# Attention scores: both row maxima of a head pair in one half step, and the next pair's score products ahead of the value products

## The chip, the cores and the metric

The kernel runs on one core of a Trainium2 chip. The metric is device time in microseconds (us) from start to end of one execution. Three executions of the kernel before took 997.72, 998.46 and 1002.0 us, so the median is 998.46 us. A fourth one was recorded by the hardware profiler, and all rows below come from it.

## The reference, cut to what matters

Three blocks follow one another: attention with a learned bias on the scores, a mixture of experts, and a dense layer with a squared ReLU. The change lies in the attention alone:

```python
# 4 batches, 8 heads, 576 positions, head size 64
scores = q @ k.T / sqrt(64) + bias[head]      # 576 x 576 for each batch and head
scores = scores - scores.max(-1)
attn = exp(scores); attn = attn / (attn.sum(-1) + 1e-9)
x = attn @ v                                  # goes on to the experts
```

## The kernel before, in words

A unit of work is a tile of 128 query rows, one batch and one pair of heads (for the last 64 rows of a batch, two batches share a tile). There are 72 units. For each unit TensorE (PE) makes four sorts of products, and three other steps lie between them:

- `emit_qk` (line 484): the score products of both heads, 12 of them for a full tile, into two PSUM tiles named `ps_s`, one for each head. The pool of these tiles holds two, so the next unit's score products cannot start before both tiles have been read.
- `emit_max` (L496), on VectorE (DVE): it reads one `ps_s`, adds the bias, writes the sum to an SBUF tile `ssb` and takes the row's extremum `mn` (with the sign turned, so that it is the row maximum of the scores). One instruction and a short read of the accumulator for each head.
- `emit_exp` (L509), on ScalarE (ACT): the exponential, from `ssb` to `pr`, one for each head.
- `emit_T` (L518) and `emit_Tx` (L523): `pr` is transposed by TensorE. Four 128x128 blocks of each head go into a bank `ps_t`; a ninth block, half of it from each head, goes into the second half of the bank `pv` (there is one such bank).
- `emit_Te` (L525 to L530): copies of `ps_t` to `pt` and of the ninth block to `pte`. The helper `copy` (L208) sends each one to ACT (L210) or DVE (L212), whichever has the smaller load counted up so far; `emit_max` and `emit_exp` add their own share to that count.
- `emit_pv` (L543): the 20 value products from `pt` and `pte` into `pv`.
- `emit_pve` (L548): the copy of the result out of `pv`, to a buffer that the rows name `big`. Only then can the next unit's ninth block be written.

The program is written out in half steps, `hs`, two for a unit (the loop from L793). In a half step the calls stand in a fixed order, and each engine runs its own instructions in the order in which they were written. A unit that starts at half step 2j has its maxima at 2j and 2j+1, its exponentials at 2j+1 and 2j+2, its transposes at 2j+3 and 2j+4, its value products at 2j+5. The score products of the next unit are written in the odd half step 2j+1, behind the value products of an older unit. So TensorE sees, unit after unit: transposes of the second head and the ninth block (even half step), transposes of the first head, value products, score products (odd half step).

Around this, background work is fed in by generators: at the front of a half step (`run(F)`) and at its end (`run(E_)`). It makes the bias (`bias_group`: products `ps_b` at L405, their copies `rt` at L317 on ACT and L319 on DVE), prepares k and q (L237, L242, L267, L272), splits expert weights (`presplit`, L455 on GpSimd and L459 on DVE) and turns finished rows (`rows`, `ps_r`, L577 to L601). Where a generator has a choice of engine or of the half step, it goes by the same load count.

Of the kernel before, what the change touches and what calls it, by code (L numbers as in the profile page):

```python
# [7 lines left out]
F32 = mybir.dt.float32  # L8
# [15 lines left out]
P = 128  # L24
# [61 lines left out]
def body(ctx: ExitStack, tc: tile.TileContext, q, k, v, wsm, emb, tau, mw1, mw2, win, wout, cst_d, lsk_d, ids_d, out):  # L86
# [44 lines left out]
    def attention(actx, bctx, cctx, smp, mid, early, G):  # L131
        ap = lambda n, bufs, **kw: actx.enter_context(tc.tile_pool(name=n, bufs=bufs, side="right", **kw))
# [1 line left out]
        bp = lambda n, bufs, **kw: bctx.enter_context(tc.tile_pool(name=n, bufs=bufs, side="right", **kw))  # L134
        kvp = ap("a_kv", 4)
        biasp = ap("a_bias", 4)
        sp_ = ap("a_s", 3)
        pp_ = ap("a_p", 2)
        ptp = ap("a_pt", 3)
        qp = ap("a_q", 4)  # L140
# [24 lines left out]
        def start(g, tag="B"):  # L165
            active.append([g, E_, tag])

        def run(where):
            for a in list(active):
                if a[1][0] == where[0]:  # L170
                    a[1] = next(a[0], None)
                    if a[1] is None:
                        active.remove(a)
# [43 lines left out]
        def V(n, extra=0.07):  # L217
            load["D"] += n * 0.00104 + extra
# [253 lines left out]
        def emit_qk(j_):  # L472
            c, pr, b = units[j_]
            parts = [(slice(0, P), b)] if c < 4 else [(slice(0, 64), b), (slice(64, P), b + 1)]
            assert all((x - x % 2, pr) in kready for _, x in parts), (j_, now)
            qd = qst[c, b]
            s = [ps.tile([P, 2, 512], F32, name="ps_s") for _ in range(2)]
            for hf in range(2):
                js = slice(hf * 288, hf * 288 + 288)
                for i, (x, y) in enumerate(((0, 0), (0, 1), (1, 0))):  # L480
                    for r, bb in parts:
                        for h2 in range(2):
                            o = slice(64 * h2, 64 * h2 + 64)
                            PE.matmul(s[h2][r, hf, :288], lhsT=qd[o, x, pr, r], rhs=kst[bb - bb % 2][o, pr, y, bb % 2, js],  # L484
                                      start=(i == 0), stop=(i == 2))
            for h2 in range(2):
                s_ps[2 * j_ + h2] = s[h2]

        mns = {}

        def emit_max(k_):
            u, h2 = units[k_ // 2], k_ % 2
            s = s_ps.pop(k_)
            mns[k_] = smp.tile([P, 1], F32, name="mn", bufs=4)
            ss = sp_.tile([P, S], F32, name="ssb")
            DVE.tensor_tensor_reduce(out=ss.rearrange("p (a j) -> p a j", a=2), in0=s[:, :, :288],  # L496
                                     in1=btile[bkey[u]][:, h2].rearrange("p (a j) -> p a j", a=2), scale=1.0 / SC,
                                     scalar=3e38, op0=ALU.add, op1=ALU.min, accum_out=mns[k_])
            V(576, 0.2)
            ssb[k_] = ss  # L500

        def emit_exp(k_):
            (c, pr, b), h2 = units[k_ // 2], k_ % 2
            if (c, b) not in sums:
                sums[c, b] = smp.tile([P, H], F32, name="sums", bufs=6)
            if h2 == 0:
                pr_sb[k_ // 2] = pp_.tile([P, 2, S], F32, name="pr")
            h = 2 * pr + h2
            ACT.activation(pr_sb[k_ // 2][:, h2], ssb.pop(k_), AF.Exp, bias=mns.pop(k_), scale=-1.0, accum_out=sums[c, b][:, h:h + 1])  # L509
            A(576, 0.28)  # L510


        def emit_T(k_):
            src = pr_sb[k_ // 2].rearrange("p h s -> p (h s)")
            pt_ps[k_] = bank("ps_t")
            for jc in range(4):
                j0 = jc * P + (640 if k_ % 2 else 0)
                PE.transpose(pt_ps[k_][:, jc * P:(jc + 1) * P], src[:, j0:j0 + P], eye)  # L518


        def emit_Tx(k_):
            x = pv_ps[k_ // 2] = pvp.tile([P, 2 * P], F32, name="pv")
            PE.transpose(x[:, P:], pr_sb.pop(k_ // 2).rearrange("p h s -> p (h s)")[:, 512:640], eye)  # L523

        def emit_Te(k_):  # L525
            pt_sb[k_] = ptp.tile([P, 4, P], F32, name="pt")
            copy(pt_sb[k_].rearrange("p a n -> p (a n)"), pt_ps.pop(k_), 512)
            if k_ % 2:
                pt_sb[k_, "e"] = ptp.tile([P, P], F32, name="pte", bufs=2)
                copy(pt_sb[k_, "e"], pv_ps[k_ // 2][:, P:], 128)  # L530

        def emit_pv(j_):
            c, pr, b = units[j_]
            pv = pv_ps[j_]
            a = [pt_sb.pop(2 * j_ + h2) for h2 in range(2)]
            e = pt_sb.pop((2 * j_ + 1, "e"))
            for j in range(1 if c < 4 else 2):
                cs = slice(0, P) if c < 4 else slice(64 * j, 64 * j + 64)
                for jc in range(5):
                    for h2 in range(2):  # L540
                        o, d = slice(h2 * 64, h2 * 64 + 64), slice(pr * 64, pr * 64 + 64)
                        vb = vt[b + j]
                        PE.matmul(pv[o, cs], lhsT=vb[:, 2 * jc + h2, d] if jc < 4 else vb[o, 8, d],  # L543
                                  rhs=a[h2][:, jc, cs] if jc < 4 else e[o, cs], start=(jc == 0), stop=(jc == 4))
# [3 lines left out]
        def emit_pve(j_):  # L548
            c, pr, b = units[j_]
            if (c, b) not in oT:  # L550
                assert free["ot"] > 0
                free["ot"] -= 1
                oT[c, b] = big[:, now_ot[0] % 4]
                now_ot[0] += 1
            copy(oT[c, b][:, pr, :], pv_ps.pop(j_)[:, :P], 128)
            if pr == NP - 1:
                if c == 4:
                    start(rows(c, b, (c, 0), b // 2, 2), "A")
                elif c == 3:
                    start(rows(c, b, (c, b // 2), b % 2, 2), "A")  # L560
                else:
                    start(rows(c, b, (c, 0), b, 4), "A")
# [192 lines left out]
        N = len(units)  # L755
# [36 lines left out]
        hs, done = HS0, 0  # L792
        while hs < 2 * N + 5:  # L793
            now[0] = G["hs"] = hs
            if hs > 113 and done == 0 and all(a[2] != "B" for a in active):
                cctx.close()
                done = 1
                mid(0)
            if done == 1 and all(a[2] != "W" for a in active):
                bctx.close()  # L800
                done = 2
                mid(1)
            if hs == -2:
                free["aux"] -= 2
            for e in load:
                load[e] = max(load[e] - STEP, 0.0)
            run(F)
            if hs < HS0 + 11:
                load["A"] = load["D"] = 0.0
            if hs < HS0 + NF:  # L810
                first(hs - HS0)
            j_ = (hs - 6) // 2
            if hs % 2 == 0 and 0 <= j_ < N:
                emit_pve(j_)
            if 0 <= hs - 3 < 2 * N:
                emit_T(hs - 3)
            if 0 <= hs - 3 < 2 * N and hs % 2 == 0:
                emit_Tx(hs - 3)
            j_ = (hs - 5) // 2
            if hs % 2 and 0 <= j_ < N:  # L820
                emit_pv(j_)
            if 0 <= hs < 2 * N:
                emit_max(hs)
            if 0 <= hs + 1 < 2 * N and hs % 2:
                emit_qk((hs + 1) // 2)
            if 0 <= hs - 1 < 2 * N:
                emit_exp(hs - 1)
            if 0 <= hs - 3 < 2 * N:
                emit_Te(hs - 3)
            run(E_)  # L830
            for f, a, g in side.get(hs, []):
                if g:
                    start(f(*a), g)
                else:
                    f(*a)
            hs += 1
# [105 lines left out]
    with tc.manual_schedule():  # L942
        lctx, ectx = ExitStack(), ExitStack()
        tp = lambda c, n, bufs, **kw: c.enter_context(tc.tile_pool(name=n, bufs=bufs, reuse_waits="tile", **kw))
        smp = ctx.enter_context(tc.tile_pool(name="sm", bufs=2))
# [9 lines left out]
        def mid(part):  # L955
            if part == 0:
                G["one"] = tp(lctx, "e_one", 1)
                G["xg"] = tp(lctx, "e_xg", 4)
                return
            G["xs"] = tp(lctx, "e_xs", 3)  # L960
            one = tp(lctx, "e_w", 1)
            w1b.append(one.tile([P, 2, 4, F1], F16, name="w1b"))
            wr1.append(one.tile([P, 4, F1], F32, name="wr1"))
            wr1.append(G["kv"].bitcast(F32)[:, :4 * F1].rearrange("p (k f) -> p k f", k=4))
# [127 lines left out]

        actx, bctx, cctx = ExitStack(), ExitStack(), ExitStack()
        tail, Q = attention(actx, bctx, cctx, smp, mid, early, G)


# [501 lines left out]
```

## Time and profile before

| What | us |
|---|---|
| three executions, median | 998.46 |
| the profiled execution, its own time | 999.73 |
| its span in the trace | 998.0 |
| from the first ninth block's transpose (42.9) to the last (377.8) | 334.9 |
| in that stretch: PE busy, DVE busy, ACT busy | 309.07, 275.78, 242.98 |

The stretch is the part of the span in which units of attention follow each other in a steady order. "Idle before" in a row is the time in which an engine did nothing just ahead of an instruction, and the arrow names what it waited for. PE's weight loads (PEld) have rows of their own; a load stands ahead of each matmul, so a wait of the queue shows there most often, and the idle time of 0.17 to 0.24 put down to "issue" is what the trace shows at a change of the kind of product where nothing was waited for.

### The profile page before, as it was taken

To read this page: it belongs to the slowest core of one execution; us is meant where nothing else is said; L and a number is where in the kernel's file an instruction comes from. 1 tells how busy PE (TensorE), PEld (TensorE's weight loads), DVE (VectorE), ACT (ScalarE), POOL (GpSimd) and SP (SyncE) were. 2 spreads that over 40 slices of the span, in tenths; PEclk is the share of its full clock that TensorE was granted. 3 is DMA by queue.
4 is the path that set the end of the run, shared out by engine and by line. 5 is a ranking of instruction groups with operands and counts; after the bars stand their busy time and mean duration, and the time that the engine had idled before them with its cause. 6 is when DMAs were issued, how large, how long until landed. Compare 5 with 4: busy or idle time off the path is not lost. (4 is left out here: it accounts for less than half of the span.)

```text
span 998.0 us, 25456 instructions
## 1 busy us (share of the span) xinstructions
PE 946.7 (95%) x10045; PEld 735.9 (74%) x10045; DVE 659.7 (66%) x1268; ACT 538.5 (54%) x992; POOL 519.5 (52%) x501
## 2 busy tenths in 40 slices
PE   8699998999999889999999999999999999999998
PEld 5366666676567668777667667688888888888887
DVE  6687898878977774677876978335455546454442
ACT  5587666777767583465665664355333323324231
POOL 0114755657634353466638787376454645454551
PEclk9799999999999999999999999999999999999999
DMA  7566955877667243698998584371111120111101
GB/s 250 211 236 226 340 187 171 278 246 256 219 205 252 88 137 133 235 346 301 342 405 319 191 292 154 116 317 43 32 54 43 28 60 16 49 43 33 33 1 43
DMA packets 71342, 172.90 MB, mean 173 GB/s; under 512 B 25032, under 2 KB 25928, under 8 KB 68624
## 3 DMA queue, kind: packets, MB, share of 16 engines
q1 hardware_dynamic: 65696, 157.24, 45.7%
q0 software_dynamic: 5520, 13.97, 4.1%
q8 instruction: 81, 1.33, 0.5%
q14 instruction: 45, 0.37, 0.1%
HBM read 171.49 MB, written 51.73 MB: 224 GB/s over the span
## 5 line engine op out<-in xcount | busy, mean ns | idle before, releaser
L1435 POOL TENSOR_TENSOR gf<-gf 128x256 f32<-128x256 f32 x144 | 166.0, 1172 | 145.6 <-DVE gf L1432 124.3
L1419 PE MATMUL pf<-big,wih 128*128 128x256 f16 x1728 | 196.0, 273 | 0.7 <-PEq L1373 0.7
L1419 PEld LDWEIGHTS <-wih 128*128 128x128 f16 x1728 | 168.9, 98 | 20.8 <-issue 1.2
L1457 PEld LDWEIGHTS <-g 128*128 128x128 f16 x1512 | 147.2, 98 | 18.9 <-issue 1.0
L1425 ACT ACTIVATE gf<-pf 128x512 f32<-128x512 f32 x72 | 42.3, 597 | 192.7 <-PE pf L1419 143.5
L1216 PE MATMUL ph<-x,w1b 128*128 128x128 f16 x2112 | 125.1, 219 | 2.9 <-ACT x L1200 1.7
L1216 PEld LDWEIGHTS <-w1b 128*128 128x128 f16 x2112 | 120.6, 98 | 7.3 <-issue 1.9
L1231 PE MATMUL py<-vt,h 128*128 128x512 f16 x528 | 119.2, 383 | 4.8 <-DMA vt<-wsc 4.7
L496 DVE CUSTOM_DVE_ANT_0 ssb<-ps_s,bias 128x576 f32<-128x576 f32 x144 | 107.8, 749 | 21.7 <-PE ps_s L484 12.9
L1443 DVE TENSOR_TENSOR g<-gf,g 128x1792 f16<-128x1792 f32 x36 | 85.5, 2375 | 47.0 <-ACT g L1442 47.0
L509 ACT ACTIVATE pr<-ssb,mn 128x576 f32<-128x576 f32 x144 | 111.9, 777 | 1.7 <-DVE mn L496 1.5
L1432 DVE TENSOR_TENSOR gf<-gf 128x1024 f32<-128x1024 f32 x28 | 34.3, 1226 | 114.2 <-ACT gf L1425 114.2
L543 PE MATMUL pv<-pt,vt 128*64 128x128 f32 (+1 forms) x1280 | 95.5, 270 | 11.5 <-ACT pte L210 4.9
L1231 PEld LDWEIGHTS <-h 128*128 128x128 f16 x528 | 51.2, 98 | 63.9 <-issue 7.6
L543 PEld LDWEIGHTS pv<-pt,vt 128*64 128x64 f32 x1280 | 70.5, 137 | 33.6 <-ACT pte L210 11.9
L518 PE MATMUL ps_t<-cst,pr 128*128 128x128 f32 x576 | 89.8, 283 | 0.7 <-DVE pl L594 0.3
L518 PEld LDWEIGHTS ps_t<-cst,pr 128*128 128x128 f32 x576 | 64.5, 144 | 27.9 <-issue 20.2
L484 PE MATMUL ps_s<-kst,qd 64*128 64x288 f16 (+1 forms) x960 | 74.9, 288 | 8.5 <-DVE mn L496 7.6
L455 POOL TENSOR_TENSOR wh<-wr,w2s_c 128x256 f16<-128x256 f32 x84 | 57.0, 708 | 49.5 <-DMA wsc<-wh 30.5
L210 ACT COPY pt<-ps_t 128x512 f32<-128x512 f32 x101 | 58.4, 578 | 24.8 <-PE ps_t L518 24.8
L484 PEld LDWEIGHTS <-qd 64*128 64x128 f16 (+1 forms) x960 | 41.6, 98 | 30.3 <-issue 13.9
L1442 ACT CAST g<-gf 128x1792 f16<-128x1792 f32 x36 | 60.3, 1676 | 4.3 <-POOL gf L1435 4.3
(200 smaller groups left out, 1569.0 us busy)
## 6 DMA issues: line engine op xcount, KB each, us to landing
vt<-wsc SPq DMA_DIRECT2D x88, 512.0 KB
wr<-in_mw_dram SPq DMA_DIRECT2D x65, 512.0 KB
kst<-in_mw_dram SPq DMA_DIRECT2D x44, 512.0 KB
wsc<-wh SPq DMA_DIRECT2D x32, 512.0 KB
bias<-bias_d SPq DMA_DIRECT2D x16, 576.0 KB
bias_d<-rt SPq DMA_DIRECT2D x28, 295.5 KB
wr<-in_win_dram SPq DMA_DIRECT2D x8, 1024.0 KB
wr<-in_wout_dram SPq DMA_DIRECT2D x8, 1024.0 KB
```

Source lines behind the costliest of these rows:

```text
L484: PE.matmul(s[h2][r, hf, :288], lhsT=qd[o, x, pr, r], rhs=kst[bb - bb % 2][o, pr, y, bb % 2, js], start=(i == 0), stop=(i == 2))
L496: DVE.tensor_tensor_reduce(out=ss.rearrange("p (a j) -> p a j", a=2), in0=s[:, :, :288], in1=btile[bkey[u]][:, h2].rearrange("p (a j) -> p ...
L509: ACT.activation(pr_sb[k_ // 2][:, h2], ssb.pop(k_), AF.Exp, bias=mns.pop(k_), scale=-1.0, accum_out=sums[c, b][:, h:h + 1])
L518: PE.transpose(pt_ps[k_][:, jc * P:(jc + 1) * P], src[:, j0:j0 + P], eye)
L543: PE.matmul(pv[o, cs], lhsT=vb[:, 2 * jc + h2, d] if jc < 4 else vb[o, 8, d], rhs=a[h2][:, jc, cs] if jc < 4 else e[o, cs], start=(jc == 0 ...
L1216: PE.matmul(p_[:, f4, :], lhsT=w[:, a, kc, f * P:(f + 1) * P], rhs=x2[:, b, kc, :], start=(i == 0), stop=(i == 11))
L1231: PE.matmul(p_, lhsT=h2[:, a, fc, :], rhs=wb2[fc // 2][:, b, fc % 2, :], start=(i == 0), stop=(i == 23))
L1419: PE.matmul(p_[:, h], lhsT=wih[:, a, kc, f * P:(f + 1) * P], rhs=y2[:, b, kc, :], start=(i == 0), stop=(i == 11))
L1435: POOL.tensor_tensor(out=g[:, d], in0=g[:, x], in1=g[:, y], op=op)
L1442: ACT.copy(gt[:, 0, :, c:c + 2, :], g[:, 1:8])
L1443: DVE.tensor_tensor(out=gt[:, 1, :, c:c + 2, :], in0=g[:, 1:8], in1=gt[:, 0, :, c:c + 2, :], op=ALU.subtract)
L1457: PE.matmul(ps, lhsT=gt[:, a, s, c, :], rhs=woh[:, c, b, w, :], start=(i == 0 and first), stop=(i == 23 and end), skip_group_check=True)
```

## The change

Both maxima of a unit are now written in its even half step, one behind the other. The score products of the next unit stay in the odd half step, but between the first head's transposes and the value products. The pool of `ssb` tiles has four buffers and that of `mn` six.

```diff
-        sp_ = ap("a_s", 3)
+        sp_ = ap("a_s", 4)
...
-            mns[k_] = smp.tile([P, 1], F32, name="mn", bufs=4)
+            mns[k_] = smp.tile([P, 1], F32, name="mn", bufs=6)
...
             if 0 <= hs - 3 < 2 * N:
                 emit_T(hs - 3)
+            if 0 <= hs + 1 < 2 * N and hs % 2:
+                emit_qk((hs + 1) // 2)
             if 0 <= hs - 3 < 2 * N and hs % 2 == 0:
                 emit_Tx(hs - 3)
             j_ = (hs - 5) // 2
             if hs % 2 and 0 <= j_ < N:
                 emit_pv(j_)
-            if 0 <= hs < 2 * N:
+            if 0 <= hs < 2 * N and hs % 2 == 0:
                 emit_max(hs)
-            if 0 <= hs + 1 < 2 * N and hs % 2:
-                emit_qk((hs + 1) // 2)
+                emit_max(hs + 1)
```

The load count now gets both maxima in the even half step and none in the odd one, so the copies and the background work are dealt out anew. Of the 144 copies `pt`, DVE has 61 where it had 43; of the 72 copies `pte`, 2 where it had 27; of the 72 copies `big`, 13 where it had 14. ACT has the others.

On PE, late in the attention where no background products lie between, one unit's round reads like this before, from the transpose of a ninth block on (`qd` and `kst` are q and k; a pair of load and product stands for twelve):

```order
L523 MATMUL pv<-cst,pr 128x128
L518 MATMUL ps_t<-cst,pr 128x128 x4
L543 MATMUL pv<-pt,vt 64x128 x8
L543 MATMUL pv<-pte,vt 64x128 x2
L484 LDWEIGHTS qd
L484 MATMUL ps_s<-kst,qd 128x288
```

And now:

```order
L523 MATMUL pv<-cst,pr 128x128
L518 MATMUL ps_t<-cst,pr 128x128 x4
L484 LDWEIGHTS qd
L484 MATMUL ps_s<-kst,qd 128x288
...
L543 MATMUL pv<-pt,vt 64x128 x8
L543 MATMUL pv<-pte,vt 64x128 x2
```

The twelve score products and the twenty value products have changed places; the next transposes follow the value products now.

On DVE in the same part of the program, two units before (an `ISA` row is a maximum, or the short read of its accumulator):

```order
L496 ISA ssb,mn<-ps_s,bias 128x576
L496 ISA mn 128x1
L212 COPY pt<-ps_t 128x512
L496 ISA ssb,mn<-ps_s,bias 128x576
L496 ISA mn 128x1
L459 SCALAR_TENSOR_TENSOR wh<-wr,wh 128x1024
L496 ISA ssb,mn<-ps_s,bias 128x576
```

And now:

```order
L496 ISA ssb,mn<-ps_s,bias 128x576
L496 ISA mn 128x1
L496 ISA ssb,mn<-ps_s,bias 128x576
L496 ISA mn 128x1
L212 COPY pt<-ps_t 128x512
L459 SCALAR_TENSOR_TENSOR wh<-wr,wh 128x1024
L496 ISA ssb,mn<-ps_s,bias 128x576
```

The two maxima stand together, and the copy `pt`, which is now that of the first head's transposes, and the weight split come behind both. In 27 units a split follows `pt` in this way before the next pair of maxima.

On DVE in the bias part, around the unit whose bias copies are 32 and 272 wide, before:

```order
L496 ISA ssb,mn<-ps_s,bias 128x576
L496 ISA mn 128x1
L310 TENSOR_SCALAR rt<-u_t,cst 128x576 x2
L319 TENSOR_SCALAR rt<-ps_b,cst 128x32
L319 TENSOR_SCALAR rt<-ps_b,cst 128x272
L496 ISA ssb,mn<-ps_s,bias 128x576
L496 ISA mn 128x1
L212 COPY pte<-pv 128x128
L496 ISA ssb,mn<-ps_s,bias 128x576
```

And now:

```order
L212 COPY pt<-ps_t 128x512
L310 TENSOR_SCALAR rt<-u_t,cst 128x576 x2
L319 TENSOR_SCALAR rt<-ps_b,cst 128x32
L319 TENSOR_SCALAR rt<-ps_b,cst 128x272
L496 ISA ssb,mn<-ps_s,bias 128x576
L496 ISA mn 128x1
L496 ISA ssb,mn<-ps_s,bias 128x576
L496 ISA mn 128x1
```

The bias copies, which wait for `ps_b`, now stand ahead of both maxima of a unit and not of one. That is so in 14 units; in 7 more a copy `big` on DVE stands there without bias copies.

## Rows read from the trace of the kernel before

**Rows 1.** Windows over the stretch from 42.9 to 377.8: sums of busy time.
```profile
sum 334.90, PE 309.07 PEld 216.17 DVE 275.78 ACT 242.98 POOL 169.06; mean PE 154.54 PEld 108.08 DVE 137.89 ACT 121.49 POOL 84.53
```

**Rows 2.** Waits from 42.9 to 378: total us, times, longest.
```profile
PEld pv L543 <- issue: 12.6, 74, 0.2
PEld L484 <- issue: 12.5, 60, 2.0
PEld pv L543 <- ACT pte L210: 11.4, 34, 1.2
PEld L484 <- DVE mn L496: 8.5, 16, 1.1
PEld pv L543 <- DVE pt L212: 7.5, 24, 1.3
PEld pv L543 <- DVE pte L212: 6.2, 17, 1.1
PEld pv L543 <- ACT pt L210: 3.5, 9, 0.6
PE pv L523 <- DVE big L212: 3.1, 8, 0.7
PE pv L523 <- ACT big L210: 2.0, 4, 0.9
```

**Rows 3.** Timeline of PEld around a wait for the maximum: start, length, instruction.
```profile
140.62 0.20 PEld L543 LDWEIGHTS pv<-pte,vt 64*64 64x64 f32 x4 [0.17 <-issue]
140.99 0.09 PEld L484 LDWEIGHTS <-qd 64*128 64x128 f16 x1 [0.17 <-issue]
141.98 0.60 PEld L484 LDWEIGHTS <-qd 64*128 64x128 f16 x11 [0.91 <-DVE mn L496]
```

**Rows 4.** Timeline of PEld in a round without background products.
```profile
283.81 0.14 PEld L523 LDWEIGHTS pv<-cst,pr 128*128 128x128 f32 x1
283.92 0.47 PEld L518 LDWEIGHTS ps_t<-cst,pr 128*128 128x128 f32 x4
284.98 0.85 PEld L543 LDWEIGHTS pv<-pt,vt 128*64 128x64 f32 x16 [0.59 <-ACT pte L210]
286.00 0.19 PEld L543 LDWEIGHTS pv<-pte,vt 64*64 64x64 f32 x4 [0.17 <-issue]
287.21 0.42 PEld L518 LDWEIGHTS ps_t<-cst,pr 128*128 128x128 f32 x4 [0.24 <-issue]
287.60 0.14 PEld L523 LDWEIGHTS pv<-cst,pr 128*128 128x128 f32 x1
```

**Rows 5.** Timeline near the start: two maxima back to back, and the products behind.
```profile
37.63 0.76 DVE L496 CUSTOM_DVE_ANT_0 ssb<-ps_s,bias 128x576 f32<-128x576 f32 x1
38.32 0.75 DVE L496 CUSTOM_DVE_ANT_0 ssb<-ps_s,bias 128x576 f32<-128x576 f32 x1
39.13 0.42 PE L484 MATMUL ps_s<-kst,qd 64*128 64x288 f16 x2 [0.28 <-DVE mn L496]
```

**Rows 6.** Timeline of a bias round: bias products, their copies, then the copy `big`.
```profile
118.67 0.64 PEld L405 LDWEIGHTS ps_b<-rt,wsb 128*32 128x32 f32 x16 [0.24 <-issue]
119.94 0.66 DVE L319 TENSOR_SCALAR rt<-ps_b,cst 128x16 f32<-128x16 f32 x2 [2.12 <-PE ps_b L405]
120.51 0.75 DVE L496 CUSTOM_DVE_ANT_0 ssb<-ps_s,bias 128x576 f32<-128x576 f32 x1
120.91 0.14 PEld L523 LDWEIGHTS pv<-cst,pr 128*128 128x128 f32 x1 [0.72 <-ACT big L210]
```

**Rows 7.** Timelines of DVE and ACT: a copy and a split; a copy behind `pv`.
```profile
138.86 0.69 DVE L212 COPY pt<-ps_t 128x512 f32<-128x512 f32 x1
139.47 1.22 DVE L459 SCALAR_TENSOR_TENSOR wh<-wr,wh 128x1024 f16<-128x1024 f32 x1
141.10 0.27 ACT L210 COPY big<-pv 128x128 f32<-128x128 f32 x1 [0.71 <-PE pv L543]
```

**Rows 8.** Groups by line and shape from 30 to 381: the copies `big` on DVE.
```profile
L212 DVE COPY big<-pv 128x128 f32<-128x128 f32 x14 | 4.0, 284 | 1.0 <-PE pv L543 1.0
```

## The prediction

> **What bounds the kernel now.** I read the windows first, to see which engine sets the pace where the change acts. In the stretch of the attention PE is busy for 309.1 of 334.9 us, DVE for 275.8 and ACT for 243.0 [rows 1]. PE is idle for 25.8 us there, 0.36 for each of 72 units; that is about what an edit that moves no work off PE can win. The other engines have slack on average, so what counts is how late their results come at PE's door.
>
> The list of waits says at which doors [rows 2]. At the value products the weight loads waited 11.4 + 7.5 + 6.2 + 3.5 = 28.6 us in 84 waits for copies of transposed blocks (`pt`, `pte`). A change of product costs 0.17 with nothing to wait for (12.6 us in 74 times), so the net loss is 28.6 - 84 x 0.17 = 14.3 us. At the score products they waited 8.5 us in 16 waits for a maximum, net of 0.21 each (12.5 in 60) 5.1 us. The ninth block's transpose waited 3.1 + 2.0 = 5.1 us in 12 waits for the copy out of the one bank `pv`.
>
> The timeline shows what such waits look like. The first score product of a unit goes at 140.99, and the next comes 0.91 us late, since the second head's maximum was not through; nothing else runs on PE meanwhile [rows 3]. In the round at 284 the value products start 0.59 us after the transposes' loads, for want of `pte` [rows 4]. Without any wait that round would be: from the value products to the next ninth block 287.60 - 284.98 = 2.62, on to the first head's transposes 0.11, their loads 0.47, a change 0.17, in all 3.37 us. The round that was measured there took 287.60 - 283.81 = 3.79.
>
> **The change, part by part.** No instruction is added or dropped but for the dealing of copies: DVE gets 18 more `pt` and 25 fewer `pte`, about 18 x 0.69 - 25 x 0.28 = +5 us with the lengths of rows 7 and 8, spread over a stretch in which it is idle for 59 us. I cost that at nothing: it hides in those 59 us; were it all on PE's path, it would be 5 us. In the lists of SP and POOL some stores of split weights now stand a place or two ahead of a bias or row store; no wait of rows 2 names a DMA or POOL, so I cost these queues at nothing too, and the price if a bias load came late for its maximum is in the range only.
>
> *Value products behind the score products.* Between the first head's transposes and the value products now lie 0.17 + 0.60 us of score products [rows 3], so the copies have 0.77 us more. The 84 waits average 0.34 with the gap, and the longest are 0.6 to 1.3. All but the longest go. I take 11.3 of the 14.3 us as won and leave 3. The ends: 14.3, or nothing if ACT, which now makes nearly all `pte` behind an exponential and a `pt`, comes later by those 0.77 us.
>
> *The broken load run.* In 24 of the 84 waits the loads stop a second time for the `pt` that DVE makes [rows 2]. DVE now makes the first head's `pt`, half a round before it is wanted, so that stop goes with its gap: 24 x 0.17 = 4.1 us. Bounds 0 and 4.1.
>
> *Both maxima early.* The second maximum no longer waits behind the background work of the even half step, so the present waits go: 5.1 us. In their place comes a new order on DVE, and it has a price, since the score products now stand one value product (about 1.2 us) nearer to their maxima. Two maxima back to back, to the point where the second head's products run, take 39.13 - 37.63 = 1.50 us [rows 5]. Three things can stand ahead of them:
>
> - A weight split behind `pt`, in 27 units. From the end of the first head's transposes: 0.28 until a copy starts (as from the end of the last loads at 140.82 to the copy at 141.10 [rows 3, 7]), 0.61 for `pt`, 1.22 for the split [rows 7], 1.50: 3.61 us. PE wants the result after one round and a change, 3.37 + 0.17 = 3.54. The loss is 0.07 each, 1.9 us; nothing where PE has background products, and up to 0.5 each (13 us) where more small work joins.
> - Bias copies, in 14 units. From the bias products' loads at 118.67 the copies start after 1.27 and the maxima after 1.84 [rows 6], so the products can go at 1.84 + 1.50 = 3.34. PE, which waits for the copy `big` there as before, is at the ninth block after 2.24, and at the score products after 0.11 + 0.47 + 0.17 more, 2.99. The loss is 0.35 each, 4.9 us; bounds 0 and, were the old wait for `big` no cover, 0.35 + 0.55 each, 12.6.
> - A copy `big` on DVE without bias copies, in 7 units. It starts 0.48 after the last four value products' loads [rows 3, 7], takes 0.28 [rows 8], then 1.50: 2.26. PE comes after 0.19 + 0.24 + 0.39 + 0.11 + 0.47 + 0.17 = 1.57 [rows 4]. The loss is 0.69, 4.8 us in all where PE has nothing else, none where bias products lie between; I take half, 2.4.
>
> *The bank `pv`.* Before, score products lay between the value products and the next ninth block; now only four transposes do. ACT's copy is done 0.48 + 0.27 = 0.75 after the last loads start [rows 3, 7], and PE is there after 0.19 + 0.24 + 0.39 = 0.82 [rows 4]. It just fits. Where ACT is behind with a background piece it doesn't: I add 1 us to the 5.1 that stay; the ends are 0 and, if half of the 59 ACT copies are 0.3 late, 9.
>
> *The extra buffers.* A third buffer would have made the second maximum wait for an exponential half a step older; the fourth takes that away. It costs nothing.
>
> The Trainium skill speaks against a cheap pair of maxima: "VectorE: DVE Perf Modes", section "The DRAIN you can't avoid", says that the next DVE operation does not start before the pipeline of the last one is empty. The rows don't show that here: the second maximum starts 0.69 after the first, whose record is 0.76 long [rows 5]. By the rule the pair would be some 0.07 longer at 48 places, which I estimate at 3 us less gain; I go by the rows.
>
> **The sum.** -11.3 - 4.1 - 5.1 + 1.9 + 4.9 + 2.4 + 1.0 = -10.3 us, against the profiled execution's own 999.73 us: 989.4. That execution lies 1.3 above the median of 998.46, which would make it 988.1. What follows the attention is untouched and simply starts earlier. I put 989.
>
> **The rivals.**
>
> *The gain is taken back on DVE.* The rows for it: DVE is busy for 82% of the stretch [rows 1], and its share falls unevenly, so that a unit with bias copies, a split and small routing work is longer on DVE than on PE. Were the 27 splits worth 0.3 (8.1), the bias units 0.55 (7.7) and the `big` ones 0.69 (4.8), the costs would be 20.6 against 20.5 won: 998, no change. Against it: rows of units in which DVE alone would set the pace are few, and its old idle time before a maximum is not needed any more.
>
> *Slower: the wait for the maxima now holds up the value products as well.* Until now a late maximum stopped PE when the value products were already through; now they stand behind it, their copies ready. This decides if the pair is late by more than about 0.5 us in most of the 48 places where something stands ahead of it: 48 x 0.6 = 29 us against 20.5 won, so about 1007. For it: the 0.91 in rows 3 with only one maximum outstanding. Against: in the new order the pair needs 1.50, and its input is there one value product earlier.
>
> *More than forecast.* If the pair is never late and ACT keeps up, all of the 20.5 us are won, and with them part of the 5.1 at the ninth block: 976 to 981. Its ceiling is PE's idle time, 998.5 - 25.8 = 973.
>
> *The change does nothing:* the score products could go first only if both maxima were through, else the order on PE is the old one in effect, and waits change their names alone. That is the first rival's time, and I count it there.
>
> **How the numbers follow.** Forecast (984 to 993.5) 0.48; more than forecast 0.14; taken back, 993.5 to 1003.5, 0.23; slower 0.15. A measurement of this kernel can tell about 0.5%, 5 us, from no change. So faster is 0.48 + 0.14 = 0.62, the same 0.23, slower 0.15. The range from 979 to 1002 leaves out the lower half of the upside (0.06) and most of the slower case (0.14). The forecast's own range is 984 to 993.5.
>
> **What the profile after would show.** Right: waits of the value products for `pte` and `pt` under 8 us in the stretch, the stretch near 324 us, hardly any wait of DVE's maxima for score products, and the rounds without background work at 3.4 to 3.6 us. The costs would show as waits of the score products for `mn` or `big`, longest in the bias units. Wrong: waits of the score products for `mn` above 15 us (the slower rival), waits of the ninth block for `big` above 12 us (the bank `pv` mis-sized), or a shorter stretch with the end no earlier, which would mean that the experts' part is tied to something other than PE's work.

## The result, and the profile after

The changed kernel took 992.01 us in the median of 5 runs (990.76 to 993.0), against 1001.96 (997.72 to 1002.38, 5 runs) for the kernel before on the same chip: a ratio of 0.9911, 95% interval 0.9887 to 0.9935. It is faster by 0.9%. The forecast was 989.0, or 1.0% less; direction and size are right. The reasons are so only in part: the price of the new order was put some 20 us too low, and gains that were put some 17 us too low hid it.

In the profiled execution the span is 990.2 us (998.0 before). The stretch from the first ninth block's transpose to the last is 43.05 to 370.2, so 327.2 us where it was 334.9. The whole gain lies there. The windows over it, which answer to [rows 1]:

```profile
sum 327.30, PE 300.82 PEld 214.09 DVE 274.11 ACT 241.29 POOL 166.10; mean PE 150.41 PEld 107.04 DVE 137.05 ACT 120.64 POOL 83.05
```

PE's idle time is 26.5 us, no less than the 25.8 of before. It is PE's busy time that fell, by 8.3 us, with the same products. I come back to that below, for the prediction took the idle time as the thing to be won.

The list of waits from 43 to 370 (total us, times, longest), which answers to [rows 2]; the first rows are the weight loads' (PEld) and the others the products':

```profile
PEld L484 <- issue: 36.5, 122, 1.3
PEld pv L523 <- ACT big L210: 5.3, 9, 1.1
PEld pv L543 <- ACT pte L210: 4.4, 16, 0.9
...
PE ps_s L484 <- DVE mn L496: 18.4, 48, 1.3
PE pv L523 <- ACT big L210: 3.0, 7, 0.8
PE pv L523 <- DVE big L212: 1.8, 5, 0.6
```

The value products' long list of waits for `pte` and `pt` has shrunk from 28.6 us in 84 to 6.1 in 22, 4.4 in 16 of it for the `pte` that ACT makes, and most of that is the gap of a change of product. The waits for `pt` made by DVE are gone. The score products, however, now wait 18.4 us for a maximum; the row of 36.5 us at their loads is the same waits seen by the load queue, with the gaps of changes in it.

A round without background work, on PEld, answers to [rows 4]:

```profile
287.54 0.14 PEld L523 LDWEIGHTS pv<-cst,pr 128*128 128x128 f32 x1
287.60 0.47 PEld L518 LDWEIGHTS ps_t<-cst,pr 128*128 128x128 f32 x4
288.24 0.61 PEld L484 LDWEIGHTS <-qd 64*128 64x128 f16 x12 [0.17 <-issue]
289.08 0.85 PEld L543 LDWEIGHTS pv<-pt,vt 128*64 128x64 f32 x16 [0.24 <-ACT pte L210]
290.11 0.20 PEld L543 LDWEIGHTS pv<-pte,vt 64*64 64x64 f32 x4 [0.17 <-issue]
290.91 0.14 PEld L523 LDWEIGHTS pv<-cst,pr 128*128 128x128 f32 x1
```

From one ninth block to the next it is 290.91 - 287.54 = 3.37 us, the 3.37 that the prediction had worked out for a round in which nothing waits; it was 3.79. Here the change does just what it was expected to do.

A round in which DVE has row work shows the new loss, on DVE, on PE and on PEld (the answer to [rows 3] and [rows 5]):

```profile
305.44 0.42 DVE L591 TENSOR_TENSOR us<-ps_r,rs 128x256 f32<-128x256 f32 x1
305.78 0.18 DVE L594 TENSOR_TENSOR pl<-ps_r,rs 128x32 f32<-128x32 f32 x1
305.88 0.75 DVE L496 CUSTOM_DVE_ANT_0 ssb<-ps_s,bias 128x576 f32<-128x576 f32 x1
306.55 0.75 DVE L496 CUSTOM_DVE_ANT_0 ssb<-ps_s,bias 128x576 f32<-128x576 f32 x1
...
305.83 0.60 PE L518 MATMUL ps_t<-cst,pr 128*128 128x128 f32 x4
306.69 0.28 PE L484 MATMUL ps_s<-kst,qd 64*128 64x288 f16 x1 [0.26 <-DVE mn L496]
307.37 0.89 PE L484 MATMUL ps_s<-kst,qd 64*128 64x288 f16 x11 [0.40 <-DVE mn L496]
...
306.36 0.09 PEld L484 LDWEIGHTS <-qd 64*128 64x128 f16 x1 [0.17 <-issue]
308.19 0.85 PEld L543 LDWEIGHTS pv<-pt,vt 128*64 128x64 f32 x16 [0.24 <-ACT pr L509]
```

The row work (1.0 us, from `run(F)`) stands ahead of the pair of maxima. The pair is through too late for PE, which stops twice, for one head and for the other, and the twelve score products are broken into 1 and 11. (The products alternate between the heads. The description of `emit_qk` above says that none can start before both tiles have been read; in fact the first one needs only the first head's tile.) The stops cost more than they show as waits: from the first load of the score products to the first of the value products it is 308.19 - 306.36 = 1.83 us here and 289.08 - 288.24 = 0.84 in the unbroken round above, so 0.99 more, where the two waits are 0.66.

There are 29 such places with 48 waits. At 9 of them row work stands right ahead of the pair (0.66 to 0.70 each, 6.0 us); at 8 it is bias copies and the bias's preparation (5.9); at 6 a copy `big` (2.0); at 6 small steps of the router and of the experts' planning, or the first splits of the experts' weights (4.6).

### The profile page after: what moved, and what is told of

Same layout as the page of the kernel before. It is cut to its first block, busy times and chain, and to the rows that moved or that the text cites. A ratio compares the mean times of both kernels' runs of the same rounds, so it can differ in the third digit from the quotient of the medians.

```text
span 990.2 us, 25509 instructions
## 1 busy us (share of the span) xinstructions
PE 937.3 (95%) x10045; PEld 733.3 (74%) x10045; DVE 658.6 (67%) x1250; ACT 536.8 (54%) x1010; POOL 515.8 (52%) x501
## 5 line engine op out<-in xcount | busy, mean ns | idle before, releaser
L496 DVE CUSTOM_DVE_ANT_0 ssb<-ps_s,bias 128x576 f32<-128x576 f32 x144 | 102.8, 751 | 5.6 <-DMA bias<-bias_d 3.8
L484 PE MATMUL ps_s<-kst,qd 64*128 64x288 f16 (+1 forms) x960 | 77.0, 289 | 19.4 <-DVE mn L496 19.0
L518 PE MATMUL ps_t<-cst,pr 128*128 128x128 f32 x576 | 90.7, 284 | 1.4 <-ACT pr L509 0.7
L518 PEld LDWEIGHTS ps_t<-cst,pr 128*128 128x128 f32 x576 | 64.7, 144 | 25.0 <-issue 17.5
L543 PE MATMUL pv<-pt,vt 128*64 128x128 f32 (+1 forms) x1280 | 81.7, 269 | 1.3 <-ACT pte L210 1.0
L543 PEld LDWEIGHTS pv<-pt,vt 128*64 128x64 f32 x1280 | 63.7, 136 | 19.1 <-issue 5.4
L484 PEld LDWEIGHTS <-qd 64*128 64x128 f16 (+1 forms) x960 | 44.7, 97 | 43.0 <-issue 37.7
L308 POOL TENSOR_SCALAR rt<-u_t,cst 128x384 f32<-128x384 f32 (+17 forms) x24 | 42.2, 1760 | 34.0 <-ACT pt L210 17.8
```

## The experiments

The runs were made in three groups, each on one chip beside the kernel before: 1010.16 us in the first group, 1001.63 in the second, 998.87 in the third. I therefore compare ratios.

**The two halves of the change alone.** First both maxima early, with the score products left behind the value products (the dealing of copies as in the changed kernel):

```diff
-            if 0 <= hs + 1 < 2 * N and hs % 2:
-                emit_qk((hs + 1) // 2)
...
             if hs % 2 and 0 <= j_ < N:
                 emit_pv(j_)
+            if 0 <= hs + 1 < 2 * N and hs % 2:
+                emit_qk((hs + 1) // 2)
```

> Both maxima in the even half step, as in the changed kernel, but the score products stay behind the value products. Theory A (the gain comes mostly from the value products' cover: the score products lie between the transposes and them): the value products still wait net 10 to 14 us for pte and pt, the score products hardly at all (under 2 us net, they waited 5.1 before), so about 4 to 5 us of the change's 9 are left: ratio to the kernel before 0.995 to 0.997. Theory B (the gain comes from the early maxima, and the order on TensorE only follows): nearly all of the gain is here, ratio 0.990 to 0.992. Theory C (the new dealing of the copies, nearly all pte on ACT, makes the gain): as B, 0.990 to 0.993, with the value products' waits gone although nothing covers them.

Measured: 1003.34 us, ratio 0.9935 (0.991 to 0.9959), between what Theories A and B expected. Run once more, beside the changed kernel on one chip:

> Early maxima with the old order on TensorE, once more beside the changed kernel. The first run of it had 35.9 us of waits (49 times) at the value products for pte and none at the score products. Theory A: the changed order on TensorE hides these, so this one is 2 to 5 us slower than the changed kernel, ratio 0.993 to 0.996. Theory B (early maxima make the gain alone): equal to the changed kernel within 1 us.

> The changed kernel itself, once more, so that the variants stand beside it on one chip. Expected: ratio to the kernel before 0.990 to 0.993, and in the stretch of the attention waits of the score products for the maxima of about 18 us (48 times), of the value products for pte and pt under 6 us, of the ninth block for big about 5 us.

Measured: 993.22 us, 0.9917 (0.9895 to 0.9939), against 992.01 us, 0.9906 (0.9887 to 0.9926), for the changed kernel. The early maxima alone give 0.8% of the 0.9%; what the new order on PE adds can't be told from nothing. This version has the new dealing of the copies too, so its 0.8% is of both; early maxima with the old order and the old dealing weren't run. Then the order alone, each maximum in its own half step as before:

```diff
+            if 0 <= hs < 2 * N and hs % 2:
+                emit_max(hs)
             if 0 <= hs + 1 < 2 * N and hs % 2:
                 emit_qk((hs + 1) // 2)
...
             if 0 <= hs < 2 * N and hs % 2 == 0:
                 emit_max(hs)
-                emit_max(hs + 1)
```

> The score products go ahead of the value products, but each maximum stays in its own half step (the second one is written at the front of the odd half step, so its place in VectorE's list is that of the kernel before), and the copies are dealt as before. Theory A: the value products' waits fall from 14 to under 5 us net, but the score products wait for a second maximum that stands behind the even half step's background work: their waits grow from 5 to 20 us or more, and the time is that of the kernel before within 5 us either way, ratio 0.997 to 1.005. Theory B: without the early maxima nothing can be won, and what the value products gain is lost twice over, ratio above 1.005. Theory C: ratio 1.00, since the dealing is that of before.

Measured: 1102.02 us, ratio 1.0922 (1.0875 to 1.0969). The list of waits of its stretch:

```profile
PE ps_s L484 <- DVE mn L496: 86.4, 76, 2.9
```

Nothing else of PE waits there for more than 2.7 us in all. Only Theory B's "above 1.005" covers it, and no theory named a loss of that size. The score products stand nearer to their maxima now, by a round's value products, the second maximum still comes in the odd half step behind the background work of the even one, and the value products, whose copies are ready, wait behind it all.

Where the time of the halves lies is read best from the weight loads grouped by line: a load stands ahead of every product, so busy plus idle-before is the time that a kind of product holds the queue. Columns: instructions, busy us, mean ns, idle before and what ended most of it. The kernel before:

```profile
L543 PEld LDWEIGHTS pv<-pt,vt 128*64 128x64 f32 x1264 | 69.5, 137 | 32.8 <-ACT pte L210 11.4 <-DVE pt L212 7.5 <-DVE pte L212 6.2
L518 PEld LDWEIGHTS ps_t<-cst,pr 128*128 128x128 f32 x569 | 63.3, 143 | 26.0 <-issue 18.8 <-PE ps_s L484 3.4 <-ACT pt L210 2.6
L484 PEld LDWEIGHTS <-qd 64*128 64x128 f16 (+1 forms) x924 | 39.2, 97 | 27.4 <-issue 12.5 <-DVE mn L496 8.5
L523 PEld LDWEIGHTS pv<-cst,pr 128*128 128x128 f32 x72 | 10.1, 140 | 8.3 <-PE ps_t L518 4.4 <-ACT big L210 3.3 <-DVE big L212 0.4
```

The early maxima alone (second run):

```profile
L518 PEld LDWEIGHTS ps_t<-cst,pr 128*128 128x128 f32 x568 | 63.0, 143 | 26.2 <-issue 16.3 <-PE ps_s L484 3.2 <-DVE mn L496 3.0
L543 PEld LDWEIGHTS pv<-pt,vt 128*64 128x64 f32 x1264 | 62.9, 137 | 39.4 <-ACT pte L210 33.1 <-issue 2.2 <-DVE pte L212 1.5
L484 PEld LDWEIGHTS <-qd 64*128 64x128 f16 (+1 forms) x924 | 37.3, 97 | 16.8 <-issue 9.6 <-DVE pt L212 0.2 <-DVE se L699 0.2
L523 PEld LDWEIGHTS pv<-cst,pr 128*128 128x128 f32 x72 | 10.2, 141 | 12.6 <-ACT big L210 9.1 <-PE ps_t L518 2.3 <-DVE big L212 1.0
```

The changed kernel:

```profile
L518 PEld LDWEIGHTS ps_t<-cst,pr 128*128 128x128 f32 x569 | 63.5, 143 | 22.4 <-issue 16.1 <-ACT pt L210 1.7 <-ACT pte L210 1.4
L543 PEld LDWEIGHTS pv<-pt,vt 128*64 128x64 f32 x1264 | 62.7, 137 | 18.4 <-issue 5.4 <-ACT pte L210 4.4 <-ACT pr L509 3.3
L484 PEld LDWEIGHTS <-qd 64*128 64x128 f16 (+1 forms) x924 | 42.5, 96 | 41.0 <-issue 36.5
L523 PEld LDWEIGHTS pv<-cst,pr 128*128 128x128 f32 x72 | 10.1, 140 | 9.9 <-ACT big L210 5.3 <-PE ps_t L518 2.3 <-DVE big L212 0.9
```

| busy + idle before, us | before | early maxima alone | changed kernel |
|---|---|---|---|
| value products from `pt` (L543) | 102.3 | 102.3 | 81.1 |
| score products (L484) | 66.6 | 54.1 | 83.5 |
| transposes (L518) | 89.3 | 89.2 | 85.9 |
| ninth block (L523) | 18.4 | 22.8 | 20.0 |
| stretch | 334.9 | 327.5 | 327.2 |

(The records of neighbouring kinds overlap a little, so the sums are not the stretch.) Early maxima win 12.5 us at the score products and lose 4.4 at the ninth block. The new order then wins 21.2 at the value products and loses 29.4 at the score products; with 3.3 and 2.8 won at the transposes and the ninth block, and 0.7 to 1.6 at each of three kinds of background product, that is about even. The changed kernel's second run, beside the early maxima on one chip, gives the same within 0.2 us at the value and the score products (81.3 and 83.5). At the value products the early maxima alone only change the names of the waits: those for DVE's `pt` are gone, and those for ACT's `pte` grew from 11.4 us to 33.1.

**The dealing of the copies.** The changed order with the load count as before, so that DVE has 43 `pt` and 27 `pte` again:

```diff
-            V(576, 0.2)
...
+            if 0 <= hs < 2 * N:
+                V(576, 0.2)
```

The first line stood in `emit_max`, the others stand in the loop, so that each half step counts one maximum.

> The changed kernel, with the load count kept as before (one maximum counted in each half step), so that DVE again has 43 pt and 27 pte where the changed kernel has 61 and 2. Theory A: order is what counts; the ratio to the kernel before is 0.990 to 0.994, with somewhat more waits of the value products (pte behind two maxima on DVE, 2 to 4 us). Theory C: the gain is lost, ratio 0.996 to 1.001.

Measured: 1003.72 us, ratio 0.9942 (0.9917 to 0.9966), beside 0.9935 for the early maxima alone on that chip; the changed kernel itself wasn't run there, and the intervals of its 0.9911 and 0.9906 elsewhere overlap with this one. The score products wait 12.9 us in 36 instead of 18.4 in 48. The ratio lies just outside what Theory A expected and further from Theory C. By the medians the dealing is worth 0.3 to 0.4%, which these runs can't tell from nothing.

**The place of the pair in the half step.** If the score products' wait is the loss, then it helps to put the pair ahead of the row work and the bias copies, at the front of the even half step:

```diff
-            V(576, 0.2)
...
+            if 0 <= hs < 2 * N and hs % 2 == 0:
+                emit_max(hs)
+                emit_max(hs + 1)
             run(F)
...
-                emit_max(hs)
-                emit_max(hs + 1)
+                V(1152, 0.4)
```

> The changed kernel, with the pair of maxima written at the very front of the even half step, ahead of the bias copies, the row work and the copy big on DVE; the copies are dealt as in the changed kernel. My account of the changed kernel is that the score products' new waits (18.4 us in 48 times) come from what stands ahead of the pair on DVE: row work, bias copies, a copy big that itself waits for the value products. If so these waits fall below 8 us and the stretch shortens by 5 to 9 us: ratio to the kernel before 0.982 to 0.987. Rival: the pair is late because DVE as a whole is late (split and pt ahead of it), then the waits stay at 14 us or more and the ratio is 0.990 to 0.993; or the waits move to the ninth block, whose pv buffer then waits for a copy big behind the pair, and the row work behind it delays banks for the transposes (ratio 0.990 or more, with over 10 us at the ninth block).

Measured: 996.72 us, ratio 0.9856 (0.9825 to 0.9888). The score products' wait fell to 3.1 us in 8, but the ninth block took over, as the waits show:

```profile
PEld pv L522 <- ACT big L210: 10.9, 13, 2.7
PEld pv L522 <- DVE big L212: 9.1, 6, 2.2
```

A copy `big` on DVE now stands behind the pair; the waits for `big` made by ACT grew as well, from 5.3 us to 10.9. Half a step earlier still, at the end of the odd half step:

> The changed kernel, with the pair of maxima written at the end of the odd half step, behind the copies pt but ahead of that half step's background work and of all that the even half step has on DVE; dealing as in the changed kernel. If what stands ahead of the pair on DVE makes the score products wait, these waits fall below 4 us. The price: background work (bias copies, row work, copies big on DVE) comes 1.5 us later. Expected like the version with the maxima at the front of the even half step, 0.983 to 0.988; if the late background work costs more than the waits, 0.990 or more, and then with more waits of the ninth block for big and of the transposes for banks.

Measured: 994.75 us, ratio 0.9928 (0.9907 to 0.995). The score products wait 2.0 us in 6, but DVE's maxima wait 14.2 us in 29 for the score products, and the ninth block 18.3. So I went back to the front of the even half step and made the copy `big` on ACT always, ahead of the background work there:

```diff
-            copy(oT[c, b][:, pr, :], pv_ps.pop(j_)[:, :P], 128)
+            ACT.copy(oT[c, b][:, pr, :], pv_ps.pop(j_)[:, :P])
+            A(128)
```

> Maxima at the front of the even half step, and the copy big beside them at the front, always on ACT, ahead of the bias copies that wait for bias products. In the version with the maxima alone at the front the waits moved in part to the ninth block: 20 us in 19 waits of its weight loads for big. If big was late because it stood behind bias copies on ACT or behind the pair on DVE, these fall below 5 us and the stretch shortens by 8 us or more against the changed kernel: ratio 0.975 to 0.983. Rival: bias copies and row work, now later, hold the banks ps_b and ps_r longer and the transposes wait for them instead: ratio 0.984 or more, with waits of the transposes above 10 us.

> No edit against the kernel with pair and copy big at the front of the even half step: run again, beside the three others, as what the order and the row work are compared with. Both theories: ratio 0.983 to 0.987, as the first time (0.985).

Measured: 986.42 us, 0.9847 (0.9826 to 0.9869), and 987.34 us, 0.988 (0.9855 to 0.9905). The loads of the ninth block wait 3.7 us for `big` in the second run, where it was 20.0 with the pair alone at the front; 10.9 us of the score products' wait came back (2.8 the longest), so the gain stayed short of the 0.975 to 0.983 that was expected. With pair and copy at the front the kernel is faster than the changed one, 986.42 us beside 992.01. The pair alone at the front has nearly the same ratio, but the changed kernel didn't run beside it; whether the copy's place adds to it can't be told, since the two ran on different chips and their intervals overlap. Last, the same kernel with the score products behind the value products again:

> Edit: as the kernel with pair and copy big at the front of the even half step, but with the score products behind the value products again, as before the change. Theory 1 (the order on PE only chooses where the wait shows, the early maxima are the gain): ratio 0.983 to 0.988, as with the new order (0.985); value products wait 25 to 35 us for pte in 45 to 55 places, score products not at all. Rival (with the maxima out of the way the new order pays, since the value products' wait is now the larger of the two, some 30 against 11 us): ratio 0.991 to 0.996, the stretch 6 to 10 us longer than 326.5.

Measured: 1006.62 us, ratio 1.0074 (1.005 to 1.0097), 19 us behind the 987.34 beside it. DVE's waits and the loads' longest, first with the score products behind, then ahead:

```profile
DVE ssb L496 <- PE ps_s L484: 38.7, 32, 4.3
PEld pv L542 <- ACT pte L210: 27.7, 38, 2.7
```
```profile
PEld pv L542 <- ACT pte L210: 8.0, 22, 1.8
DVE ssb L496 <- PE ps_s L484: 2.9, 5, 1.2
```

Both theories missed the size: none, or 6 to 10 us. With the pair at the front of the half step the place of the score products counts: with them last on PE, DVE stands still at the pair in 32 rounds, and all of DVE's later work with it.

**The row work alone.** The rest of the score products' wait in the changed kernel is tied to what DVE does ahead of the pair. This kernel moves one such thing. It holds the row products back to the end of an even half step, so that DVE's part of them comes in an odd one (PE's row products move with it):

```diff
             yield from take("aux", 2)
+            while now[0] % 2:
+                yield E_
             pr_ = Q["aux"]("ps_r")
```

> Edit: the changed kernel, but the products of the row work are held back to the end of an even half step, so that its VectorE part (about 1.1 us) falls at the front of an odd one and no longer stands ahead of the pair of maxima. In the changed kernel that is so at 9 of the 31 places where score products wait, 0.66 us each, 6.0 of 18.4 us. Theory 1 (the row work ahead of the pair is the missing term, and its wait is a real loss): the score products' waits for mn fall to 11 to 13 us, the stretch from about 326.7 to 320 to 323, ratio 0.984 to 0.987 (changed kernel 0.991). Rival (the time comes back as a wait elsewhere, at the ninth block or for the copies): the waits for mn fall as much, but the ninth block or the value products wait 4 us longer, the stretch stays at 326 to 328, ratio 0.989 to 0.993.

Measured: 981.17 us, ratio 0.9816 (0.979 to 0.9841), the fastest version of all. It beats the kernel before and the changed kernel (0.9911 and 0.9906; the intervals lie apart). The list of waits and the loads at the score products:

```profile
PE ps_s L484 <- DVE mn L496: 9.3, 26, 1.0
```
```profile
L484 PEld LDWEIGHTS <-qd 64*128 64x128 f16 (+1 forms) x924 | 40.4, 96 | 30.1 <-issue 25.2
```

The nine places with 6.0 us (of 29 in all, where the expectation says 31) are gone; with what shifted at the others the wait fell by 9.1 us, to 26 waits at 18 places, and the score products by 83.5 - 70.5 = 13.0. The stretch is 315.1 us, 12 shorter (11.5 shorter than that of the kernel with three buffers, below, on the same chip). About 1 us each came back at the value products, the transposes and the ninth block, and the moved row products themselves hold the load queue for 2.7 us less, so not all of the gain is the maxima's. Theory 1 has the direction and the place right; the gain is larger than the 4 to 7 us that it expected, which counted the waits alone and not the broken runs. Whether moving the row work would also speed up the pair at the front, or the old order on PE, wasn't tried.

**Three buffers for `ssb`.**

```diff
-        sp_ = ap("a_s", 4)
+        sp_ = ap("a_s", 3)
```

> Edit: the changed kernel with three buffers for ssb instead of four. Theory 1 (what the prediction says of the buffers: the second maximum then waits for an exponential of half a step before): VectorE's maxima wait for ACT's pr in 10 or more places, over 8 us, ratio 0.996 to 1.003. Rival (that exponential has long run when the second maximum comes, half a round later): hardly a wait for pr, under 2 us, ratio 0.989 to 0.993, as with four.

Measured: 992.12 us, ratio 0.9922 (0.9898 to 0.9946), as with four. In the stretch one maximum waits 0.8 us for an exponential, and so it does with four. The fourth buffer is worth nothing that can be measured.

## Why the prediction was right, and where its steps failed

*Direction and size.* Forecast -10.3 us on the profiled execution; the stretch fell by 7.7 us and the median of the comparison by 10. The time is inside the forecast's own range.

*Value products behind the score products, and the broken load run.* Forecast -11.3 and -4.1. Measured at that line: 102.3 to 81.1, so -21.2. The mechanism is as described (the waits are below the 8 us that were set as the mark, those for DVE's `pt` gone, and with the order left as it was there is no gain at that line), and the two terms together were 6 too small.

*Both maxima early, the old waits.* Forecast -5.1. The early maxima alone take 12.5 off the score products, so the term was less than half of what it is. It was read from the load queue's row for `mn` [rows 2], with the gap of a change taken off each wait. But a wait behind the first of the twelve products, as in [rows 3], is a second stop besides the change, so nothing was to be taken off; and the row "issue" of the same line, longest 2.0 us, held waits too.

*Both maxima early, the new order's price.* This is the step that failed. Forecast +1.9 (splits), +4.9 (bias copies) and +2.4 (copy `big`), 9.2 in all. Measured: a wait of 18.4 us, and 29.4 us more at the score products' line than with the maxima early and the old order. The prediction listed three things that can stand ahead of the pair. Row work is not among them, nor are the router's steps and the experts' first splits, but for the "small work" in the bound of the splits; these are 10.6 of the 18.4 us. The things on the list waited 5.9 (bias) and 2.0 (`big`), not far from their terms, and a split of `presplit` stands right ahead of the pair at none of the 29 places. The other 11 us of the price lie beyond the waits, and for that the prediction had no term; broken runs account for most of it if the 0.33 us of the round above stands for all 29 places. Moving the row work alone took 11 us off the time (981.17 beside 992.12 with the three buffers), so this was a real loss.

*What hid the failure.* The gains were forecast too small by 6 (value products), by 7 (old waits) and by 3 (transposes, not forecast at all), the price by some 20. The sum came out within 3 us all the same. That the new order on PE is what wins, as the largest term had it, fell: the early maxima alone give nearly all, and the order gives it back where it takes it. But it isn't worthless. Without the early maxima it costs 9%, with the pair at the front of the half step it is worth 1.9%.

*The bank `pv`.* Forecast +1.0; measured +1.6 at that line, and 4.8 us of waits where it was 5.1. The size is right by luck. The term was put down to the new order, but the early maxima alone cost 4.4 there, and the new order gave 2.8 back.

*The extra buffers.* That the fourth costs nothing is right. That a third would have made the second maximum wait is wrong.

*The rivals.* "Slower" set its mark at a wait above 15 us, and the wait was 18.4. The mechanism was there, at 29 places with about 0.6 us each, though only 14 of these have right ahead of the pair a bias piece or a `big`. Its price of 29 us is even what the score products' line shows (29.4); it didn't decide, since the gains were larger than thought. "Taken back on DVE" names the same loss. "More than forecast" took PE's idle time as a ceiling, and so did the opening of the prediction; the last section shows that it is none.

*The end of the stretch.* The span fell by 7.8 us where the stretch fell by 7.7, so what follows did start earlier.

*The rule on back-to-back operations.* The paragraph of the Trainium skill that the prediction draws on ("VectorE: DVE Perf Modes", section "The DRAIN you can't avoid") also says that a next operation which is not held starts earlier. So the 0.07 us a pair did not follow from it without asking whether the second maximum is held. The trace agrees with the earlier start: 306.55 - 305.88 = 0.67 us, with a record of 0.75.

## What to carry to other kernels

When an instruction is moved ahead on a queue, list everything that its producer's engine may run ahead of it, background work too, and price the whole list. A late producer can cost more than its wait, since it also breaks a run of products (0.99 us for 0.66 here). When both a consumer and its producer are moved, try each alone. Here one half gives nearly everything, the other alone costs 9%, and a third edit (the row work in the other half step) doubles the gain.

## What the runs showed of the hardware

PE's idle time was no ceiling. The same 1008 full value products took 81.3 us of busy time before and 69.3 after, with 280 and 279 ns each, as the groups of PE's products show (before, then after):

```profile
L543 PE MATMUL pv<-pt,vt 128*64 128x128 f32 x1008 | 81.3, 280 | 9.7 <-ACT pte L210 4.1 <-DVE pte L212 1.7 <-ACT pt L210 1.1
```
```profile
L543 PE MATMUL pv<-pt,vt 128*64 128x128 f32 x1008 | 69.3, 279 | 0.9 <-ACT pte L210 0.6 <-DVE pte L212 0.3
```

One run of sixteen shows where it went: the products of before as PE has them, and their loads.

```profile
139.22 1.47 PE L543 MATMUL pv<-pt,vt 128*64 128x128 f32 x16
```
```profile
139.22 0.19 PEld L543 LDWEIGHTS pv<-pt,vt 128*64 128x64 f32 x2 [0.17 <-ACT pte L210]
139.60 0.84 PEld L543 LDWEIGHTS pv<-pt,vt 128*64 128x64 f32 x14 [0.19 <-DVE pt L212]
```

And after:

```profile
289.08 1.09 PE L543 MATMUL pv<-pt,vt 128*64 128x128 f32 x16
```

The loads stop behind the second one, PE's row shows 1.47 us of unbroken work instead of 1.09, and the 0.38 count as busy. Such stops are to be looked for on PEld. With the row work moved the stretch is 19.8 us shorter than before, and PE is still idle for 17 of its 315 us.

In the kernel with the order alone PE waited for 86 us at the score products, and the mean granted clock was lower as well, 0.92 over its stretch where it was 1.00; the mean weight load of a value product took 156 ns there and 137 before, and PE's busy time was 337.6 us where it was 309.1. So its 9% is not waiting alone; how much of it is the clock wasn't separated.
